# Attention in chunks of 64 tokens of two batches, in front of a gated MoE, on one core

## The chip, the core and the metric

The kernel runs on one core of a Trainium2 chip. The metric is the device time of one execution in microseconds (us), from runs on the chip; the profile is one execution more, recorded by the hardware profiler. The engines are TensorE (PE, and PEld for its weight loads), VectorE (DVE), ScalarE (ACT), GpSimd (POOL) and SyncE (SP, which issues the DMAs).

## The reference

Per batch and head a 48x48 state decays and grows with each token, and is read by the query. The result of all heads is a row of 384 numbers per token, which goes through two matrix products with a gate between.

```python
B, H, S, D = 4, 8, 768, 48
for t in range(S):
    state = alpha[:, :, t, :, None] * state + np.einsum('bhd,bhe->bhde', k[:, :, t], v[:, :, t])
    y[:, :, t] = np.einsum('bhd,bhde->bhe', q[:, :, t], state)
x = y.transpose(0, 2, 1, 3).reshape(B * S, H * D)      # 3072 x 384
h = x @ w_in                                           # 384 x 2048
g = h * tanh(softplus(h))
out = g @ w_out                                        # 2048 x 384
```

All is float32; the MoE weights arrive as 64-bit words and are taken apart on the chip.

## The kernel before

**Work.** The 3072 tokens are 24 chunks of 128 tokens of one batch, ordered by position and then batch, so chunk n continues the state of chunk n - 4. A MoE unit is one block f of 128 of the 2048 hidden columns for 2 or 4 chunks: nine matmuls up (`up`, L820, a float32 product as three passes over high and low parts), seven element-wise steps on ScalarE and VectorE (L829 to L855), and three matmuls down per chunk (`down`, L883), summed in a PSUM bank of the chunk. `SEGMENTS` fixes the order of the 106 units: 20 units of 2 chunks for chunks 0 to 7 and blocks 0 to 4, then units of 4 chunks. Units 20 to 24 are chunks 4 to 7 with blocks 5 to 9, units 25 to 35 chunks 0 to 3 with blocks 5 to 15, 36 to 41 chunks 4 to 7 with blocks 10 to 15, and from 42 on chunks 8 to 23. `weight` (L409) takes each of the 16 weight blocks apart, for w_in and w_out, on VectorE (L430, L435, L440, L459) and ScalarE (L445); for the first three blocks TensorE helps (L469, L470).

**A chunk of attention** (`attention`, L514). Four pairs of heads lie in 112 partitions: one head in rows 0 to 47, the other in rows 64 to 111. VectorE makes decay products by two scans (`scan_rest` L561, `scan_front` L578), scales the keys in two parts (`mult_k` L573) and the queries (`mult_q` L588), and decays the state (`decay` L593). TensorE makes the scores (`scores` L608): of the 128x128 causal square of each head only three 64x64 blocks, by 16 products of 48 rows in quarters of the array, half of them 128 and half 64 columns wide. VectorE copies the causal part to `probs` (`mask` L618), twice a chunk, 384 columns each. TensorE turns the keys by four transposes (`turn` L756), ScalarE copies them (L760). `product` is the y block: the past (state times queries, L633, 8 products of 48 rows and 128 columns in quarters), the late half's diagonal (L633, 8 products of 128 rows and 64 columns), the change of the state (L660, 8 products of 128 rows and 48 columns) and the early half's diagonal (L633, 8 products of 64 rows and 64 columns). Each float32 product is two instructions. A memset on GpSimd (L647) stands between the past and the early diagonal. The first chunk of a batch has no past, the last no turn and no change of state.

**After the y block.** ScalarE writes the high part of x (`upper` L687), VectorE the low part (`lower` L692); for chunks below `X_PE` = 8, TensorE subtracts (`off` L699) and ScalarE copies (`left` L707) instead. Six small DMAs a chunk move rows of x (`move` L713). VectorE adds the change to the state (`gather` L794), or ScalarE copies it in the first chunks (L792). A finished chunk's result goes from PSUM through ScalarE (`result` L917) into one store (L923). At the end a sum over all checks decides whether a general path must run (L996, L997).

**The order of the work** is written by a planner, `Plan.order` (L176): every task has an engine, a cost, a key and needs. An engine takes, of the tasks it may look at (`WINDOW`), the one that can begin first, and among equals the one with the lowest key. The keys come from due times (`due`, counted in units) and the tables `SHIFT`, the costs from `COST`. PSUM has eight banks: two "att", two "h" for `up`, and o0 to o3; `EARLY_BANKS` lends h and o banks to some chunks. q, k and alpha have two buffers, `rest` one. Where TensorE would wait before a planned time of 130 us, the planner puts in dummy matmuls (`fill`, L933).

## Time and profile before

| | |
|---|---|
| time, median of 3 runs | 509.16 us (509.13 to 509.31) |
| profiled execution, span from first to last instruction | 507.4 us |
| TensorE clock granted | 0.997 of full |
| instructions | 11433 |
| moved by DMA | 56.68 MB, mean 112 GB/s |

The profiled execution has no time of its own beside its span; the runs are 1.8 us above it, which is what lies before the first and behind the last instruction. In the rows, an engine's busy time counts overlapping matmuls once, and a matmul's length runs from its start to the end of its pipeline, so neighbours overlap: what a stretch of matmuls costs is read from its start to the start of the next one. A row with `x16` merges 16 instructions.

### The profile page before, as it was taken

What the parts mean: (1) busy time and instruction counts of PE and PEld (TensorE: products, weight loads), DVE (VectorE), ACT (ScalarE), POOL (GpSimd) and SP (SyncE); (2) the same over time, 40 slices, a digit from 0 to 9 for tenths busy, and PEclk for the clock granted to TensorE, in tenths of its full rate; (3) what the DMA queues carried; (4) which work ended last, traced back from release to release, by engine and by line L of the source; (5) the groups of instructions that cost most, each with busy time, mean ns of one, the idle gap of its engine ahead of it and who ended that gap; (6) DMA issues with size and microseconds to landing.
All of it is one profiled execution on the core that took longest, in us unless ns stands there. A gap on an engine that the chain in (4) does not pass through costs nothing.

```text
span 507.4 us, 11433 instructions
## 1 busy us (share of the span) xinstructions
PE 499.2 (98%) x4453; PEld 439.0 (87%) x4453; DVE 377.6 (74%) x729; ACT 391.1 (77%) x908; POOL 4.7 (1%) x34
## 2 busy tenths in 40 slices
PE   7999999999999999999999999999999999999996
PEld 4678899988988888889988888988989988999996
DVE  8999999999998897878557477867467654454442
ACT  2567799979879899969966955858866866887774
POOL 2000000000000000000000000000000000000000
PEclk9999999999999999999999999999999999999998
DMA  8656542525316685763220150220032000100001
GB/s 324 239 200 199 166 151 80 175 92 175 125 63 211 218 271 192 242 235 122 83 69 33 63 167 8 85 84 5 30 122 83 4 10 8 64 0 1 1 1 66
DMA packets 20074, 56.68 MB, mean 112 GB/s; under 512 B 4016, under 2 KB 12464, under 8 KB 20016
## 3 DMA queue, kind: packets, MB, share of 16 engines
q1 hardware_dynamic: 20016, 55.91, 32.4%
q8 instruction: 36, 0.59, 0.5%
q14 instruction: 22, 0.18, 0.1%
HBM read 48.82 MB, written 4.72 MB: 106 GB/s over the span
## 4 chain that ended last, share of the span: by engine, by line
PE 94%; DVE 4%; issue 1%; POOL 1%; ACT 0%; POOLq 0%
PE bank L883 40%; PE bank L820 40%; PE bank L633 7%; PE bank L608 3%; PE bank L660 2%; PE bank L756 1%; DVE rest L561 1%; DVE qka L578 1%; DVE probs L618 1%; PE bank L933 1%; DVE w_lead L435 0%; DVE qka L588 0%; PE bank L699 0%; PE bank L469 0%; DVE w_lead L440 0%
## 5 line engine op out<-in xcount | busy, mean ns | idle before, releaser
L883 PE MATMUL bank<-wo,g 128*128 128x384 f32 x1152 | 218.1, 339 | 0.0
L820 PE MATMUL bank<-xs,wi 128*128 128x512 f32 (+1 forms) x954 | 212.5, 372 | 0.1
L883 PEld LDWEIGHTS bank<-wo,g 128*128 128x128 f32 x1152 | 199.1, 188 | 5.6 <-issue 0.3
L820 PEld LDWEIGHTS bank<-xs,wi 128*128 128x128 f32 x954 | 167.0, 188 | 28.9 <-PE bank L883 0.4
L839 DVE SCALAR_TENSOR_TENSOR y<-u,bank 128x512 f32<-128x512 f32 (+1 forms) x106 | 66.8, 632 | 47.0 <-ACT u L829 46.8
L855 DVE TENSOR_TENSOR g<-t,g 128x512 fp32r<-128x512 f32 (+1 forms) x106 | 66.4, 637 | 32.3 <-ACT g L852 31.9
L852 ACT ACTIVATE g<-t 128x512 fp32r<-128x512 f32 (+1 forms) x106 | 60.8, 586 | 29.8 <-PE bank L883 26.5
L848 DVE SCALAR_TENSOR_TENSOR t<-y,t 128x512 f32<-128x512 f32 (+1 forms) x106 | 67.0, 634 | 21.4 <-ACT t L845 21.1
L829 ACT ACTIVATE u<-bank 128x512 f32<-128x512 f32 (+1 forms) x106 | 58.3, 550 | 30.2 <-PE bank L820 29.4
L842 ACT ACTIVATE t<-t,tenth 128x512 f32<-128x512 f32 (+1 forms) x106 | 71.6, 677 | 1.5
L835 ACT ACTIVATE t<-u 128x512 f32<-128x512 f32 (+1 forms) x106 | 62.0, 587 | 10.4 <-DVE g L855 9.6
L845 ACT ACTIVATE t<-t 128x512 f32<-128x512 f32 (+1 forms) x106 | 61.7, 584 | 0.7
L561 DVE TENSOR_TENSOR_SCAN rest<-qka,behind 112x516 f32<-112x516 f32 x24 | 29.5, 1228 | 1.9 <-DMA qka<-in_qka_dram 1.8
L618 DVE COPY_PREDICATED probs<-causal,bank 128x384 f32<-128x384 uint32 x48 | 25.9, 584 | 5.5 <-PE bank L608 5.5
L578 DVE TENSOR_TENSOR_SCAN qka<-qka,ahead 112x516 f32<-112x516 f32 x24 | 29.4, 1225 | 0.0
L687 ACT ACTIVATE xs<-bank 112x256 fp32r<-112x256 f32 x48 | 16.2, 378 | 15.6 <-PE bank L633 10.7
L633 PE MATMUL bank<-probs,v 128*64 128x64 f32 (+3 forms) x768 | 26.9, 227 | 0.2
L633 PEld LDWEIGHTS bank<-probs,v 128*64 128x64 f32 (+3 forms) x768 | 20.6, 128 | 6.3 <-issue 3.1
L608 PE MATMUL bank<-qka 48*64 48x128 f32 (+1 forms) x768 | 21.2, 248 | 0.2 <-DVE qka L588 0.2
L608 PEld LDWEIGHTS bank<-qka 48*64 48x64 f32 x768 | 18.2, 133 | 3.7 <-issue 1.9
L829 ACT ACTIVATION_READ_ACCUMULATOR u<-bank 128x1 f32 x106 | 20.6, 194 | 0.0
L573 DVE TENSOR_TENSOR qka<-qka,rest 112x256 f32<-112x256 f32 x48 | 19.2, 404 | 0.0
(79 smaller groups left out, 323.9 us busy)
## 6 DMA issues: line engine op xcount, KB each, us to landing
qka<-in_qka_dram SPq DMA_DIRECT2D x22, 770.5 KB, 4.8
ws<-in_wp_dram SPq DMA_DIRECT2D x16, 768.0 KB, 4.4
wc<-in_wp_dram SPq DMA_DIRECT2D x16, 768.0 KB, 4.7
v<-in_vp_dram SPq DMA_DIRECT2D x24, 192.0 KB, 4.5
out_dram<-osb SPq DMA_DIRECT2D x16, 192.0 KB, 1.9
xs<-xs SPq DMA_DIRECT2D x144, 16.0 KB, 2.1
out_dram<-part SPq DMA_DIRECT2D x8, 192.0 KB, 2.0
qka<-in_qka_dram SPq DMA_DIRECT2D x2, 258.5 KB, 3.5
```

What stands on the lines that cost most here:

```text
L608: nc.tensor.matmul(p[a][to, i, blocks], K()[r : r + D, j, to], q.rearrange("p (x t) -> p x t", t=HALF), start=True, stop=True,)
L633: return nc.tensor.matmul(p[m][64 * side : 64 * side + wide, j % 2, t], l(wide), r, start=j % 2 == 0 and lead, stop=stop, skip_group_check ...
L820: nc.tensor.matmul(p[:, :N], wi[:, z, s, fs], x[:, s, :, a], start=m == 0, stop=m == len(passes) - 1,)
L829: nc.scalar.activation(wide(u), wide(h), AF.Exp, scale=-1.0, accum_out=uchk[:, at : at + 1])
L835: nc.scalar.activation(wide(t), wide(u), AF.Square, bias=1.0, scale=2.0)
L839: nc.vector.scalar_tensor_tensor(wide(y), wide(u), 0.5, wide(h), ALU.add, ALU.mult)
L842: nc.scalar.activation(wide(t), wide(t), AF.Ln, bias=tenth, scale=0.1)
L845: nc.scalar.activation(wide(t), wide(t), AF.Exp, scale=-1.0)
L848: nc.vector.scalar_tensor_tensor(wide(t), wide(y), 0.4, wide(t), ALU.mult, ALU.mult)
L852: nc.scalar.activation(g.tile[:, 0, :N], wide(t), AF.Copy)
L855: late[mybir.EngineType.DVE] = nc.vector.tensor_tensor(g.tile[:, 1, :N], wide(t), g.tile[:, 0, :N].bitcast(F32), ALU.subtract)
L883: made = nc.tensor.matmul(o.tile[:, :DM], g.tile[:, a, j * C : (j + 1) * C], wo[:, z, f], start=begins and m == 0, stop=end and m == 2,)
```

## The change

A chunk is now 64 tokens of each of two batches; there are still 24 chunks of 128 rows, but two chains of 12 in place of four of 6, so chunk n continues chunk n - 2. The two batches' states lie side by side (384 columns in place of 192).

- Scores: two diagonal 64x64 blocks per pair and head, 16 products of 48 rows and 64 columns. Half of the past (`past(1)`, 8 products of 48 rows and 64 columns) is put in front of them, so scores now need the decayed state.
- y block: 16 diagonal products of 64 rows and 64 columns, the other half of the past (`past(0)`, 8 products), and 16 products of 64 rows and 48 columns for the change of the state. All are quarters of the array. The GpSimd memset is gone; the first diagonal product depends on the two masks.
- Banks: three a chunk instead of five. The two y banks hold scores, past, products and the change of the state; chunks 0 to 3 keep scores apart.
- VectorE: masks of 256 columns, keys in one instruction, decay of 384 columns, the state's change added in two pieces of 192. `X_PE` is 4.
- Each finished chunk is stored by two DMAs of 64 rows.
- The tables `EARLY_BANKS`, `SHIFT` and `COST` have new values, and `WINDOW` is 10**6.

Cut to its core; the functions' removed lines stand in the listing above.

```diff
...
-NCH = S // C
-QKA = (3 * C + 1) * NPAIR + 1
+NX = B // 2
+NBLK = S // HALF
+NSEG = 2 * NPAIR
+SEG = HALF + 1
+QKA = 2 * NPAIR * C + NSEG * SEG + 1
...
-    0: "o3 h att att o1".split(),
-    1: "att o0 o2 att att".split(),
+    0: "att o3 att h att".split(),
+    1: "o2 att h h att".split(),
...
-X_PE = 8
+X_PE = 4
...
-WINDOW = 150
+WINDOW = 10**6
...
+    "load v": (0.47, 0.82), "load w": (0.45, 2.51), "move": (0.6, 0.15), "store": (0.94, 0.75),
...
+    "state": (0.275, 0.4), "state0": (0.28, 0.35), "decay": (0.475, 0.6), "mask": (0.36, 0.5),
+    "scores0": (0.7, 0.8), "scores": (0.95, 1.05), "y0": (1.2, 1.3), "y": (1.45, 1.55),
+    "y last": (1.0, 1.1), "turn": (0.35, 0.58),
...
-    chunks = [(b, c) for c in range(NCH) for b in range(B)]
+    chunks = [(p, c) for c in range(NBLK) for p in range(NX)]
...
-    for b in range(B):
-        t = const.tile([R, NPAIR * D + P // 2 - D], F32, name=f"state{b}")
+    for b in range(NX):
+        t = const.tile([R, NSEG * D + P // 2 - D], F32, name=f"state{b}")
...
-        banks = EARLY_BANKS.get(n, ["att"] * 5)
-        bufs = [bank(z) for z in banks[:4]]
-        sc_buf, y_buf = bufs[:2], bufs[2:]
-        Q = lambda: by_pair(q_buf.tile[:R, : NPAIR * C])
-        K = lambda: by_pair(q_buf.tile[:R, NPAIR * C : 2 * NPAIR * C])
+        banks = EARLY_BANKS.get(n, ["att"] * 3)
+        y_buf = [bank(z) for z in banks[1:3]]
+        sc_buf = [bank(z) for z in banks[3:5]] or y_buf[::-1]
+        Q = lambda: by_half(q_buf.tile[:R, : NPAIR * C])
+        K = lambda: by_half(q_buf.tile[:R, NPAIR * C : 2 * NPAIR * C])
...
-        def mult_k(m):
-            def part():
-                k = K()[:, 2 * m : 2 * m + 2].rearrange("p j (x s) -> p j x s", x=2)
-                past = by_pair(rest.tile[:, 1:])[:, 2 * m : 2 * m + 2, 1:]
-                past = past.rearrange("p j (x s) -> p j x s", x=2)
-                nc.vector.tensor_tensor(k, k, past[:, :, :: -1 if m else 1], ALU.mult)
-            return part
+        def mult_k():
+            k = by_seg(q_buf.tile[:R, NPAIR * C : 2 * NPAIR * C])
+            nc.vector.tensor_tensor(k, k, by_seg(rest.tile[:, 1:])[:, :, 1:], ALU.mult)
 
...
+        of_state = st[:, : NSEG * D].rearrange("p (n e) -> p n e", n=NSEG)
+        by_head = st[:, : NSEG * D].rearrange("p (j x e) -> p j x e", j=NPAIR, x=2)
 
         def decay():
             nc.vector.tensor_tensor(
-                by_head, by_head, total().broadcast_to([R, NPAIR, D]), ALU.mult
-            )
+                of_state, of_state, total().broadcast_to([R, NSEG, D]), ALU.mult
+            )
+
+        SC = 2 * C
+        rows = lambda z: slice(HALF * z, HALF * z + D)
+        summed = lambda x: by_pair(within(y_buf[x])[:, :SC])
+        of_scores = lambda a: by_pair(within(sc_buf[a])[:, SC:])
+        change = lambda x: within(y_buf[x])[:, SC : SC + NPAIR * D].rearrange(
+            "p (j e) -> p j e", j=NPAIR
+        )
+
+        def head(j, a, x, start, weights, moving, stop=False):
+            side = 1 ^ a ^ (j // 2)
+            wide = D if side else HALF
+            return nc.tensor.matmul(
+                summed(x)[HALF * side : HALF * side + wide, j], weights(wide), moving,
+                start=start, stop=stop, skip_group_check=True,
+            )
+
+        def past(apart):
+            for i in range(2):
+                for j in (i, i + 2):
+                    for a in range(2):
+                        x, r = a ^ apart, rows(a)
+                        at = (2 * j + x) * D
+                        head(
+                            j, a, x, bool(apart) and i == 0, lambda w: st[r, at : at + w],
+                            Q()[r, j, x],
+                        )
 
         def scores():
...
+            if not first:
+                past(1)
+            leads = first or sc_buf[0] is not y_buf[1]
+            for j in range(NPAIR):
+                for x in range(2):
+                    for a in range(2):
                         nc.tensor.matmul(
...
+                            of_scores(a)[HALF * x : HALF * x + HALF, j], K()[rows(a), j, x],
+                            Q()[rows(a), j, x], start=leads and j == 0, stop=True,
+                            skip_group_check=True,
                         )
 
         slot = [(2 * n + a) % len(probs) for a in range(2)]
+        masked = [None, None]
 
         def mask(a):
             def part():
...
+                masked[a] = nc.vector.copy_predicated(probs[slot[a]], causal4, of_scores(a))
             return part
 
         def product():
...
+            leads = first and sc_buf[0] is not y_buf[1]
+            for i in range(2):
+                for a in range(2):
+                    for j in (i, i + 2):
+                        h = (2 * j + a) * D
+                        for x in range(2):
+                            part = slice(HALF * x, HALF * x + HALF)
+                            made = head(
+                                j, a, x, leads and i == 0 and a == 0,
+                                lambda w: V()[part, h : h + w], probs[slot[a]][part, j],
+                                stop=first and i == 1,
+                            )
+                            if i == j == a == x == 0:
+                                for z in masked:
+                                    tc.add_manual_dep(
+                                        made.ins, z.ins.name, SYNCED, reason="rows apart"
+                                    )
             if not first:
...
+                past(0)
+            if not last:
+                leads = sc_buf[0] is y_buf[1]
+                for j in range(NPAIR):
+                    for x in range(2):
+                        part = slice(HALF * x, HALF * x + HALF)
+                        for a, wide in ((0, HALF), (1, D)):
+                            h = (2 * j + a) * D
+                            nc.tensor.matmul(
+                                change(x)[HALF * a : HALF * a + wide, j],
+                                ks_buf.tile[part, j, HALF * a : HALF * a + wide],
+                                V()[part, h : h + D], start=leads and j == 0, stop=True,
+                                skip_group_check=True,
                             )
...
...
-        of = lambda m: by_slot(y_buf[m].tile)[:R]
-        to = lambda m, z: x[:R, 2 * m : 2 * m + 2, place, z]
+        of = lambda m: summed(m)[:R]
+        to = lambda m, z: x[:R, :, place, z, HALF * m : HALF * m + HALF]
...
-        t_k = [
-            add(
-                "DVE", *COST["half mult"], key + 0.03, mult_k(m), [t_rest, got_k], [q_buf, rest],
-                port=True,
-            )
-            for m in range(2)
-        ]
+        t_k = add("DVE", *COST["mult"], key + 0.03, mult_k, [t_rest, got_k], [q_buf, rest], port=True)
...
-        t_sc = add("PE", *COST["scores"], key + 0.2, scores, [*t_k, t_q], [q_buf, *sc_buf], small=(True, True))
+        t_sc = add(
+            "PE", *COST["scores0" if first else "scores"], key + 0.2, scores, [t_k, t_q, *t_decay],
+            [q_buf, *y_buf] + ([] if sc_buf[0] is y_buf[1] else sc_buf), small=(True, True),
+        )
...
-            [*t_mask, t_q, got_v, *t_decay] + ([] if last else [t_ks]),
-            [q_buf, v_buf, *y_buf] + ([] if last else [ks_buf]), small=(not first, True),
+            [*t_mask, t_q, got_v] + ([] if last else [t_ks]),
+            [q_buf, v_buf, *y_buf] + ([] if last else [ks_buf]), small=(True, True),
...
-        def gather():
-            u = y_buf[0].tile[:R, 2 * C : 2 * C + NPAIR * D].rearrange("p (j e) -> p j e", j=NPAIR)
-            if first:
-                nc.scalar.copy(by_head, u)
-            else:
-                nc.vector.tensor_tensor(by_head, u, by_head, ALU.add)
+        def gather(x):
+            def part():
+                u = change(x)[:R]
+                if first:
+                    nc.scalar.copy(by_head[:, :, x], u)
+                else:
+                    nc.vector.tensor_tensor(by_head[:, :, x], u, by_head[:, :, x], ALU.add)
+            return part
 
         done_state[b] = [
             add(
-                *(("ACT", *COST["state0"]) if first else ("DVE", *COST["state"])), key + 0.7,
-                gather, [t_y], [y_buf[0]],
-            )
+                *(("ACT", *COST["state0"]) if first else ("DVE", *COST["state"])),
+                key + 0.7 + 0.01 * x, gather(x), [t_y], [y_buf[x]],
+            )
+            for x in range(2)
         ]
-
 
...
-                nc.sync.dma_start(out[ds(b * S + c * C, C), :], osb.tile)
+                for x in range(2):
+                    nc.sync.dma_start(
+                        out[ds((2 * b + x) * S + c * HALF, HALF), :],
+                        osb.tile[HALF * x : HALF * x + HALF],
+                    )
...
+        a = inputs[name].reshape(NX, 2, NPAIR, 2, NBLK, HALF, D).transpose(3, 0, 4, 6, 2, 1, 5)
...
+    vp = inputs["v"].reshape(NX, 2, H, NBLK, HALF, D).transpose(0, 3, 1, 4, 2, 5)
+    vp = np.ascontiguousarray(vp).reshape(NX, NBLK, P, H * D)
...
```

## Rows read from the trace of the kernel before

**Rows 1.** The page, busy time and share of the span by engine.
```profile
PE 499.2 (98%) x4453; PEld 439.0 (87%) x4453; DVE 377.6 (74%) x729; ACT 391.1 (77%) x908; POOL 4.7 (1%) x34
```

**Rows 2.** The page, chain that ended last, shares by engine.
```profile
PE 94%; DVE 4%; issue 1%; POOL 1%; ACT 0%; POOLq 0%
```

**Rows 3.** Busy by stage: stage and length; PE, PEld, DVE, ACT, POOL; clock; DMA.
```profile
33.00:107.00 74.00, 73.85 (x828) 67.86 (x818) 72.28 (x170) 63.34 (x186) 0.35 (x4) 1.00 0.46 153
107.00:190.00 83.00, 83.00 (x744) 72.87 (x743) 77.13 (x152) 74.73 (x169) 0.49 (x4) 1.00 0.51 173
190.00:420.00 230.00, 229.84 (x2068) 204.12 (x2067) 158.27 (x280) 174.98 (x386) 1.06 (x12) 1.00 0.27 90
```

**Rows 4.** Timeline of PE: start, length, line, operation, count.
```profile
106.75 2.24 PE L820 MATMUL bank<-xs,wi 128*128 128x512 f32 x9
...
262.39 0.66 PE L633 MATMUL bank<-qka,state 48*48 48x128 f32 x16
262.98 0.68 PE L633 MATMUL bank<-probs,v 128*64 128x64 f32 x16
263.47 0.64 PE L660 MATMUL bank<-v,ks 128*48 128x48 f32 x16
264.04 0.46 PE L633 MATMUL bank<-probs,v 64*64 64x64 f32 x16
264.42 2.35 PE L883 MATMUL bank<-wo,g 128*128 128x384 f32 x12
```

**Rows 5.** Chain that ended last, in order of time, merged: start, length, what.
```profile
256.86 0.39 PE bank L756 x4
...
259.34 0.81 PE bank L608 x24
...
371.06 1.58 PE bank L633 x40
372.64 0.67 PE bank L608 x24
```

**Rows 6.** The same chain at an early chunk's two subtractions.
```profile
52.71 0.23 PE bank L699 x2
```

**Rows 7.** Groups of PE by shape: busy, mean ns, idle before.
```profile
L633 PE MATMUL bank<-probs,v 64*64 64x64 f32 x192 | 10.9, 230 | 0.0
```

**Rows 8.** Groups of DVE by shape: busy, mean ns, idle before.
```profile
L618 DVE COPY_PREDICATED probs<-causal,bank 128x384 f32<-128x384 uint32 x48 | 25.9, 584 | 5.5 <-PE bank L608 5.5
L573 DVE TENSOR_TENSOR qka<-qka,rest 112x256 f32<-112x256 f32 x48 | 19.2, 404 | 0.0
L588 DVE TENSOR_TENSOR qka<-qka 112x512 f32<-112x512 f32 x24 | 16.4, 683 | 0.0
L692 DVE TENSOR_TENSOR xs<-bank,xs 112x256 fp32r<-112x256 f32 x32 | 12.5, 417 | 5.1 <-ACT xs L687 5.1
L593 DVE TENSOR_TENSOR state<-state,rest 112x192 f32<-112x192 f32 x20 | 7.0, 350 | 0.0
L794 DVE TENSOR_TENSOR state<-bank,state 112x192 f32<-112x192 f32 x16 | 5.7, 356 | 5.3 <-PE bank L633 3.4 <-ACT xs L687 1.4 <-PE bank L699 0.6
```

**Rows 9.** Groups of PE by shape in the first 106.7 us.
```profile
L820 PE MATMUL bank<-xs,wi 128*128 128x256 f32 x180 | 24.6, 286 | 0.0
...
L820 PE MATMUL bank<-xs,wi 128*128 128x512 f32 x36 | 9.0, 393 | 0.0
```

**Rows 10.** Timeline of DVE: chunk 8's first scan, weight block 9's w_in part.
```profile
70.98 1.22 DVE L561 TENSOR_TENSOR_SCAN rest<-qka,behind 112x516 f32<-112x516 f32 x1
...
103.83 0.56 DVE L459 TENSOR_TENSOR wi<-w_lead,wi 128x384 fp32r<-128x384 f32 x1
```

**Rows 11.** The last stores: timeline, then line L923 (min/median/max ns of one issue).
```profile
501.67 1.89 SPq L923 DMA_DIRECT2D out_dram<-osb  x4
...
L923 SPq DMA_DIRECT2D out_dram<-osb x16: 332/333/714, 281.4 to 503.2; - x16
```

**Rows 12.** Groups of ACT by shape: busy, mean ns, idle before.
```profile
L829 ACT ACTIVATE u<-bank 128x512 f32<-128x512 f32 x86 | 50.7, 590 | 26.2 <-PE bank L820 25.4
```

194 lines of the change are left out of this document (59 added, 135 removed), and 39 rows, old and new, of the table SHIFT.

## The prediction

> **What bounds the kernel now.** I read the page's busy shares first [rows 1], then the chain of waits [rows 2], then the busy time by stage [rows 3]. TensorE is busy 98% of a span of 507.4 us, and the chain that ended last lies on TensorE for 94% and on VectorE for 4%. The stages tell where VectorE matters: between 33 and 107 us TensorE is busy 73.85 of 74 us, but VectorE also 72.28 of 74; between 107 and 190 VectorE has 77.13 of 83; from 190 to 420 it has 158.27 of 230, while TensorE is still full [rows 3]. So from about 107 us on, a microsecond less on TensorE is a microsecond less of time; before that, it is so only if VectorE can keep up.
>
> How a chunk of attention stands on TensorE is read from one chunk in the middle [rows 4] and from the merged chain [rows 5]. Scores take 0.81 us. The y block is four stretches: past (16 instructions, start 262.39), diagonal of the late half (262.98), state change (263.47), and the 64x64 diagonal (264.04), until the next MoE matmul starts at 264.42: 2.03 us. I fit these with one unit. Past and the 64x64 stretch have the same 16 instructions in four quarters, four rounds each, with 128 columns in one and 64 in the other: 0.59 against 0.38 us. The difference, 0.21 us over 4 rounds, is 0.053 us for a round of 64 columns, and 0.38 - 4 x 0.053 = 0.17 us is left as the price of one stretch of a shape. It gives 12 x 0.053 + 0.17 = 0.81 for the scores (4 rounds of 128 columns, 4 of 64), as measured, and 16 x 0.053 + 0.17 = 1.02 for the two 128-row stretches, against 264.04 - 262.98 = 1.06. Where 64x64 products were followed by scores, these took 0.67 [rows 5]: no 0.17 between 64-row and 48-row quarters.
>
> **The change on TensorE.** Everything becomes quarters, so scores and y are one stretch each. Middle chunk: scores now hold half of the past (8 products, 4 rounds) and 16 products of 64 columns (8 rounds): 12 x 0.053 + 0.17 = 0.81. The y block holds 16 diagonal products (8 rounds), the other half of the past (4) and 16 of the state change (8; 48 columns, taken at the full 0.053 since weights are up to 64 wide): 20 x 0.053 + 0.17 = 1.23. Together 2.04 against 0.81 + 2.03 = 2.84. First chunks: 8 and 16 rounds, 0.59 + 1.02; before, 0.81 and a y without past, 16 + 4 rounds and two stretches, 1.40. Last chunks: 0.81 + 12 rounds, 0.81; before 0.81 + 1.58 [rows 5].
> - Before: 24 x 0.81 + 4 x 1.40 + 16 x 2.03 + 4 x 1.58 = 63.8 us.
> - After (2 first, 20 middle, 2 last): 2 x 1.61 + 20 x 2.04 + 2 x 1.62 = 47.3 us: **-16.5**.
> - Two more chunks turn their keys (22, not 20) at 0.39 [rows 5]: +0.8.
> - X_PE 4 instead of 8: four chunks drop two subtractions each, 0.23 a chunk [rows 6]: -0.9.
>
> Sum -16.6, of which chunks 0 to 7 have 8 x 0.81 + 4 x 1.40 + 4 x 2.03 - (2 x 1.61 + 6 x 2.04) = 4.7 and the 0.9, so 5.6; chunks 8 to 23 have **11.0**. The number of returns from attention to MoE is the same, so they cancel.
>
> One rule speaks against this. The 32 score instructions in 0.81 us are 25 ns each, but the 64x64 stretch has a length of 0.46 with a mean instruction of 0.230 [rows 4, 7], so its 16 starts fit in 0.23 us, 15 ns apart; I take the rounds. The Trainium skill, "TensorE: Matmul & The Clock Gate", section "Wait — 56ns, not 53.3ns?", says that starts never come closer than about 25 ns however small the matmul; by that the middle chunk would have 128 instructions, 3.2 us. The trace's 15 ns contradict that for quarters.
>
> **The change on VectorE**, all prices from [rows 8]. For chunks 0 to 7:
> - keys: one 112x512 (0.683) for two 112x256 (2 x 0.404): 8 x -0.125 = -1.0.
> - masks of 256 columns for 384, twice a chunk. Not shown; bounds are 0.584 (no gain) and two thirds, 0.389. The 512- and 192-column rows differ by 0.333 over 320 columns, about 1.04 ns each, so 0.45: 16 x -0.135 = -2.2.
> - decay, 384 columns for 192, in six chunks instead of four. Bounds 0.350 and 0.683; by that slope 0.55: 6 x 0.55 - 4 x 0.35 = +1.9.
> - state change added in two pieces of 192, in six chunks instead of four: (12 - 4) x 0.356 = +2.8.
> - remainder of x for chunks 4 to 7, moved here from TensorE and ScalarE: 8 x 0.417 = +3.3.
>
> Together **+4.8 us** before the MoE units need it. Does it show? By 106.7 us, 20 half and 4 full units of MoE have begun: 180 and 36 up matmuls [rows 9]; the next, unit 24, begins at 106.75 [rows 4]. It needs the w_in part of weight block 9, which VectorE ends at 103.83 + 0.56 = 104.4 [rows 10]. TensorE alone would bring unit 24 to 106.75 - 5.6 = 101.1; VectorE alone to 104.4 + 4.8 = 109.2. But VectorE has already done chunk 8's preparation there (its scan runs at 70.98), whose result MoE needs only after 190: two scans, keys, q and decay, 2 x 1.22 + 2 x 0.40 + 0.68 + 0.35 = 4.3 us [rows 8, 10]. An order made anew can put that later: 109.2 - 4.3 = 104.9, so unit 24 comes **1.8 earlier**. I take this value, between 5.6 earlier and 2.5 later.
>
> After 107 us the added VectorE work (0.55 - 0.35 + 0.356 - 2 x 0.135 - 0.125 = 0.16 a middle chunk) goes into its idle time, 72 us between 190 and 420 [rows 3]. ScalarE loses eight evictions and gets nothing. POOL's memset between the two row halves goes; its wait covered nothing. Scores now also wait for decay; decay waits for the state of two chunks earlier, but the double-buffered q/k/alpha load already waits for that chunk's products, so it adds little. If that cover fails, score blocks and the mask queue behind them slip, and MoE units already prepared run in the gap.
>
> **The end.** Each result goes out in two stores: eight in place of four on SyncE after the last matmuls. Before, four take 1.89 us [rows 11], paced by ScalarE's results; one issue takes at least 0.332, and eight at some 0.4 end about 0.9 later: **+0.9** (0 to 1.5). The other 40 go into SyncE's idle time.
>
> **Sum.** Profile and runs differ by what lies around the span: 507.4 against a median of 509.16, so 1.8 us, unchanged. 509.2 - 11.0 - 1.8 + 0.9 = 497.3; I say **497.3**.
>
> **Rivals.**
> - VectorE keeps up everywhere, TensorE's whole saving shows: 509.2 - 16.6 + 0.9 = 493.5. For: the chunk 8 work done too early; against: 72.28 of 74 us. Chance 0.18.
> - VectorE sets the pace to unit 24 with nothing moved: 509.2 - 11.0 + 2.5 + 0.9 = 501.6. Chance 0.14.
> - Banks: y banks now hold scores, past and products until the state is gathered, so the table lends MoE's "h" banks oftener for longer; each loan can make one up wait for the two steps that free the other bank, the exponential (0.59 [rows 12]) and a VectorE step of 512 columns (0.68 [rows 8]). At some 10 loans, 12 us: about 509. Against: VectorE idles later [rows 3]. Chance 0.02.
> - The other side, the change not doing what it says: quarters don't overlap four wide, starts come 25 ns apart as the scores' mean has it [rows 4, 5]. Middle chunks cost 128 x 0.025 = 3.2, first ones 2.4, last ones 2.4: 2 x 2.4 + 20 x 3.2 + 2 x 2.4 = 73.6 against 63.8, so 509.2 + 9.8 + 0.8 - 0.9 + 0.9 = 519.8. It decides from 2.84 / 128 = 22 ns on. Against: 15 ns [rows 4, 7]. The page of the Trainium skill named above would have it so. Chance 0.04.
>
> The forecast itself keeps 0.62. Low end: 493.5 and up to 3 us from a new order in the first 33 us, 490.5. High end: 501.6 and dearer quarters; the diff's own cost table gives 0.93 + 2.13 - 0.95 - 1.45 = 0.66 a middle chunk where I have 0.80, 20 x 0.14 = 2.8: 504.4. A measurement of this kernel can tell about 0.2%, 1 us. Faster: all but the last two rivals and a little, 0.93; same 0.02; slower 0.05.
>
> **What would show it.** Right: scores stretch near 0.8 and y block near 1.2 us to the next MoE start, one stretch without the 0.17 gaps; VectorE nearly full to 105 us and unit 24 near 105; TensorE full after that; VectorE's total near 385 us. Wrong: starts in quarters over 20 ns apart, TensorE idle before up matmuls on "h" banks, idle time after 107 us, or unit 24 after 109 us.

## The result: 512.55 us, 0.6% slower, and the profile after

The changed kernel takes a median of **512.55 us** (511.8 to 513.16, four runs) against 509.24 for the kernel before: ratio 1.0062, interval 1.0048 to 1.0076. Forecast were 497.3 us, range 490.5 to 504.4, and 0.93 for faster. The profiled execution took 512.09 us, with a span of 510.4.

The page's busy shares and the chain that ended last, answering to [rows 1, 2]:

```profile
PE 493.4 (97%) x5251; PEld 433.8 (85%) x5251; DVE 382.7 (75%) x738; ACT 388.5 (76%) x902; POOL 2.4 (0%) x12
...
PE 82%; DMA 6%; DVE 5%; ACT 3%; issue 2%; SPq 1%; DVEq 0%
```

TensorE has 5.8 us less to do and the span is 3 us longer. Before, the chain lay on TensorE for 94% and touched no DMA; now 6% of it, some 31 us, are transfers.

The stages of [rows 3] (stage and length; PE, PEld, DVE, ACT, POOL; clock; DMA):

```profile
33.00:107.00 74.00, 73.36 (x989) 67.59 (x990) 73.07 (x176) 63.66 (x183) 0.00 (x0) 1.00 0.46 151
107.00:190.00 83.00, 81.18 (x879) 72.13 (x877) 77.74 (x152) 69.09 (x157) 0.00 (x0) 1.00 0.43 138
190.00:420.00 230.00, 226.61 (x2487) 200.84 (x2487) 161.94 (x286) 180.50 (x396) 0.00 (x0) 1.00 0.32 105
```

From 107 to 420 us TensorE now idles 5.2 us, where it idled 0.2. The clock is full in every stage; it plays no part.

Attention itself, in TensorE's timeline (start, length, line, count), answering to [rows 4]. L605 holds past, diagonal and head products, L628 the scores, L669 the state change, L879 the down products:

```profile
226.45 0.46 PE L605 MATMUL bank<-qka,state 48*48 48x64 f32 x16
226.71 0.66 PE L628 MATMUL bank<-qka 48*64 48x64 f32 x32
227.30 1.34 PE L879 MATMUL bank<-wo,g 128*128 128x384 f32 x6
...
238.49 0.69 PE L605 MATMUL bank<-probs,v 64*48 64x64 f32 x32
238.97 0.44 PE L605 MATMUL bank<-qka,state 48*48 48x64 f32 x16
239.20 0.67 PE L669 MATMUL bank<-v,ks 64*48 64x48 f32 x32
239.80 1.49 PE L879 MATMUL bank<-wo,g 128*128 128x384 f32 x7
```

Scores take 227.30 - 226.45 = 0.85 us (forecast 0.81), y 239.80 - 238.49 = 1.31 (1.23): 2.16 a middle chunk, 2.04 forecast, 2.84 before. 128 matmul instructions in 2.16 us start 17 ns apart on average, so quarters do overlap, and the rival of 25 ns is out.

So the saving is real. To see where it went I added up, over all matmuls of a trace, the time from its start to the next one's start, and gave it to its line; MoE and weight products at their undisturbed pace (up 0.229 us for 512 columns, down 0.174, dummy 0.164), what they took beyond it as "waits and switches". The third column is the kernel half_stores_half_check of below, in which the stalls are gone.

| us on TensorE, from its first matmul to the first one behind the last down | before | after | stalls taken away |
|---|---|---|---|
| attention (of it ahead of 33 us) | 63.3 (9.1) | 52.4 (6.4) | 50.6 (6.4) |
| dummies | 9.0 | 13.9 | 13.9 |
| turns of keys | 7.8 | 8.3 | 7.9 |
| subtractions of x | 2.6 | 1.9 | 1.9 |
| MoE and weight products | 404.4 | 404.4 | 404.4 |
| waits and switches of shape | 13.9 | 19.6 | 16.6 |
| sum | 501.0 | 500.5 | 495.5 |

Attention lost 10.8 us, 2.7 of them ahead of 33 us, where nothing is gained: the first up product starts at 32.92 us instead of 33.14, and dummies fill the place. Their group in the first 33 us, in the kernel before and after:

```profile
L933 PE MATMUL bank<-behind 112*128 112x384 bf16 x51 | 12.3, 376 | 2.6 <-DVE behind L349 2.6
```
```profile
L933 PE MATMUL bank<-behind 112*128 112x384 bf16 x79 | 16.8, 355 | 2.4 <-DVE behind L352 2.4
```

The last down ends at 502.00 us, before at 502.58 (first row; the second is the changed kernel's): of all that was saved 0.6 us is left there.

```profile
494.10 8.48 PE L883 MATMUL bank<-wo,g 128*128 128x384 f32 x48
```
```profile
493.49 8.51 PE L879 MATMUL bank<-wo,g 128*128 128x384 f32 x48
```

And then the end loses 3.6: 510.4 - 502.0 = 8.4 us from the last down to the span's end, before 507.4 - 502.58 = 4.8. SyncE's timeline there, answering to [rows 11]:

```profile
501.08 5.71 SPq L920 DMA_DIRECT2D out_dram<-osb  x8
```

Eight stores take SyncE 5.71 us from the first to the last, where four took 1.89. Seven of the eight issues take 0.47 to 0.60 us, the last 1.36; the four of before took 0.33 each and waited for ScalarE's results in between.

The other loss is between 165 and 215 us. SyncE's queue (L920 stores, L490 loads for the weight check, L533 and L542 a chunk's q/k/alpha and v, L709 moves of x), first in the kernel before, then after:

```profile
177.36 1.51 SPq L923 DMA_DIRECT2D out_dram<-part  x3
...
191.57 7.57 SPq L488 DMA_DIRECT2D wc<-in_wp_dram  x3
203.00 1.37 SPq L923 DMA_DIRECT2D out_dram<-part  x2
```
```profile
173.20 5.05 SPq L920 DMA_DIRECT2D out_dram<-part  x6
...
193.15 10.62 SPq L490 DMA_DIRECT2D wc<-in_wp_dram  x3
203.95 5.74 SPq L920 DMA_DIRECT2D out_dram<-part  x8
209.79 0.53 SPq L490 DMA_DIRECT2D wc<-in_wp_dram  x1
210.43 0.37 SPq L533 DMA_DIRECT2D qka<-in_qka_dram  x1
```

A row of the queue counts SyncE's waits between its issues too. The issues alone, as count and min/median/max ns, are these in the same stretch, before and then after:

```profile
L923 SPq DMA_DIRECT2D out_dram<-part x8: 343/392/525, 177.4 to 210.5; - x8
```
```profile
L920 SPq DMA_DIRECT2D out_dram<-part x16: 467/541/942, 173.2 to 209.2; - x16
```

Eight issues of 128 rows sum to 3.3 us, sixteen of 64 rows to 9.0: a store of half the rows holds SyncE longer, not shorter. The weight check loads wait for their buffer in the same queue, and the next chunk's q/k/alpha stands behind both.

A wait costs the queue more still. In both traces each of SyncE's DMAs (251 before, 275 after) signals on the semaphore of the DMA eight places ahead of it, and is not issued until that one has landed. So a queue with twice as many stores reaches less far ahead in the work. The q/k/alpha load at 187.16 us follows the landing, at 187.10, of the one issued at 178.98, eight places ahead, after 2.4 us without an issue. Between 165 and 220 us SyncE's waits of this kind are these (us in total, times, longest) and one of 0.2:

```profile
SPq L533 <- DMA qka<-in_qka_dram: 3.6, 2, 2.3
SPq L920 <- DMA wc<-in_wp_dram: 1.8, 2, 1.5
SPq L542 <- DMA v<-in_vp_dram: 1.2, 1, 1.2
SPq L709 <- DMA qka<-in_qka_dram: 1.0, 1, 1.0
```

Together they are 7.8 us; the kernel before has none there. (A check load's wait for the load whose buffer it takes, 4.5 us and before 4.0, is not counted.) What all that does is in the chain and then in TensorE's timeline (bracket: idle time before, and what ended it):

```profile
180.54 7.03 DMA v<-in_vp_dram
...
193.15 5.54 DMA wc<-in_wp_dram
...
203.45 5.76 DMA wc<-in_wp_dram
209.23 0.99 ACT wc L499 x2
```
```profile
211.09 0.57 PE L750 MATMUL bank<-ident,qka 112*128 112x112 f32 x4 [1.16 <-DVE xs L688]
```

A late check load holds ScalarE, which is in order, at its check (L499); what ScalarE should do behind it, x for the next MoE units (L683), comes late, and TensorE idles.

### The profile page after: what moved, and what is told of

The parts are those of the page before. It is cut to its first block, busy times and chain, and to the rows that moved or that the text cites. A ratio compares the mean times of both kernels' runs of the same rounds, so it can differ in the third digit from the quotient of the medians.

```text
span 510.4 us, 13018 instructions
## 1 busy us (share of the span) xinstructions
PE 493.4 (97%) x5251; PEld 433.8 (85%) x5251; DVE 382.7 (75%) x738; ACT 388.5 (76%) x902; POOL 2.4 (0%) x12
## 4 chain that ended last, share of the span: by engine, by line
PE 82%; DMA 6%; DVE 5%; ACT 3%; issue 2%; SPq 1%; DVEq 0%
PE bank L816 35%; PE bank L879 33%; PE bank L605 4%; PE bank L933 3%; DMA qka<-in_qka_dram 3%; DMA wc<-in_wp_dram 2%; PE bank L628 2%; PE bank L750 2%; PE bank L669 1%; DMA v<-in_vp_dram 1%; PE bank L471 1%; SPq L709 1%; DVE rest L559 1%; DVE y L835 1%; DVE qka L568 1%
## 5 line engine op out<-in xcount | busy, mean ns | idle before, releaser
L879 PE MATMUL bank<-wo,g 128*128 128x384 f32 x1152 | 219.4, 339 | 1.2 <-DVE g L851 0.8
L879 PEld LDWEIGHTS bank<-wo,g 128*128 128x128 f32 x1152 | 200.6, 188 | 7.8 <-DVE g L851 1.6
L559 DVE TENSOR_TENSOR_SCAN rest<-qka,behind 112x520 f32<-112x520 f32 x24 | 29.7, 1236 | 6.6 <-DMA qka<-in_qka_dram 6.6
L572 DVE TENSOR_TENSOR_SCAN qka<-qka,ahead 112x520 f32<-112x520 f32 x24 | 29.6, 1235 | 0.0
L683 ACT ACTIVATE xs<-bank 112x256 fp32r<-112x256 f32 x48 | 15.8, 378 | 13.9 <-PE bank L669 5.7
L605 PE MATMUL bank<-qka,state 48*48 48x64 f32 (+1 forms) x704 | 20.2, 222 | 0.6 <-DVE y L835 0.3
L605 PEld LDWEIGHTS bank<-qka,state 48*48 48x48 f32 (+1 forms) x704 | 15.4, 127 | 5.8 <-issue 4.2
L933 PE MATMUL bank<-behind 112*128 112x384 bf16 x85 | 18.0, 353 | 2.4 <-DVE behind L352 2.4
L639 DVE COPY_PREDICATED probs<-causal,bank 128x256 f32<-128x256 uint32 x48 | 18.9, 442 | 0.7 <-PE bank L628 0.5
L605 PEld LDWEIGHTS bank<-probs,v 64*48 64x48 f32 (+1 forms) x768 | 13.4, 127 | 6.4 <-issue 2.2
L688 DVE TENSOR_TENSOR xs<-bank,xs 112x256 fp32r<-112x256 f32 x40 | 15.2, 418 | 3.2 <-ACT xs L683 3.1
```

Source lines behind the costliest of these rows:

```text
L559: nc.vector.tensor_tensor_scan(t[:, :0:-1], alpha()[:, :0:-1], behind[:, ::-1], 0.0, ALU.mult, ALU.max)
L605: return nc.tensor.matmul(summed(x)[HALF * side : HALF * side + wide, j], weights(wide), moving, start=start, stop=stop, skip_group_check= ...
L879: made = nc.tensor.matmul(o.tile[:, :DM], g.tile[:, a, j * C : (j + 1) * C], wo[:, z, f], start=begins and m == 0, stop=end and m == 2,)
```

## The experiments

**Theory A**: the doubled stores in SyncE's queue turned the saving round. **Theory B**: the new order put the loads for the weight check where they stall the queue; the stores matter only at the end. Runs 8 to 12 look for a store without the fault, 13 and 14 price it in the change itself, 15 to 17 ask what is left when the order is made anew.

**1. one_store.** A chunk's result in one DMA.

```diff
-for x in range(2):
-    nc.sync.dma_start(out[ds((2*b+x)*S + c*HALF, HALF), :], osb.tile[HALF*x : HALF*x+HALF])
+to = out.rearrange("(z s) d -> z s d", s=S)[2*b : 2*b+2]
+nc.sync.dma_start(to[:, c*HALF : c*HALF+HALF], osb.tile)
```

> The changed kernel with one store for a finished chunk, 128 rows with the two batches' 64 rows as two pieces of one DMA; the order of all other work is the same. Theory A (the second store of each chunk clogs SyncE's queue): the eight last stores of the changed kernel hold SyncE from 501.08 to 506.79 us, the four of the kernel before ended at 503.56, so about 2.7 us come back at the end, and most of the slip of some 6 us between 165 and 215 us too, where loads of q/k/alpha and v stand behind stores: 503.5 to 506 us in all. Theory B (the new order puts weight-check loads, chunk loads and moves too close together, whatever the stores do): only the end comes back, 509 to 510.5 us.

555.19 us, ratio 1.0889 (1.0859 to 1.0919). Both theories missed. SyncE's timeline shows four such stores, and the DMA view from 212.7 to 221.4 us, in 40 slices, the busy share of the 16 engines in tenths and GB/s:

```profile
212.67 8.71 SPq L920 DMA_DIRECT2D out_dram<-part  x4
```
```profile
DMA  0994458969998322021111111111111111111411
GB/s 0 132 198 113 113 226 339 367 254 367 395 424 339 141 113 85 35 85 71 57 56 42 56 42 56 42 56 42 56 56 42 56 42 56 42 57 42 132 49 49
```

While only stores are under way, about a tenth of the engines' time is used, some 50 GB/s. The Trainium skill, "DMA: Bandwidth & Descriptors", section "Why a DMA increments its semaphore by 16 and not by 1", says that a DMA uses the largest number of engines, up to 16, that divides the slowest dimension of both its patterns; here one of them is 2, and 2 of 16 agrees with the row. A store in a poor shape is worse than two in a good one, and later versions put 64 outermost.

**2. half_check_loads** and **3. before_two_stores.** The first loads and checks only the w_in half of a weight block; the second is the kernel before with each store in two.

```diff
# half_check_loads
-t.rearrange("p m c w -> p (m c w)"),
-w[f].rearrange("p m c -> p (m c)").bitcast(I32),
+t.rearrange("p m c w -> p (m c w)")[:, : 2 * DM],
+w[f].rearrange("p m c -> p (m c)").bitcast(I32)[:, : 2 * DM],
...
# before_two_stores
-nc.sync.dma_start(out[ds(b*S + c*C, C), :], osb.tile)
+for x in range(2):
+    nc.sync.dma_start(out[ds(b*S + c*C + x*HALF, HALF), :], osb.tile[x*HALF : x*HALF+HALF])
```

> The changed kernel with the weight check loading and checking only the w_in half of each block (384 KB instead of 768 KB; the check of w_out is left out), two stores as they are. Theory A: the loads are not the cause, within 1.5 us of the changed kernel's 512.55. Theory B: the loads of 5.5 us that ScalarE and SyncE's queue wait for between 165 and 215 us are halved and the slip goes: 506.5 to 508.5 us.

> The kernel before with each store cut into two DMAs of 64 rows, nothing else. Theory A: the end grows by 2.7 us as in the changed kernel, and SyncE's queue is fuller in the middle, where this kernel had little slack between 190 and 210 us: 512 to 516 us. Theory B: only the end grows, 511.5 to 512.5 us.

half_check_loads: 507.31 us (0.9976, 0.995 to 1.0002), 5.2 less than the change. before_two_stores: 516.25 (1.0136, 1.0119 to 1.0153), 7.0 more than the kernel before. The same rows in each, last down products and last stores:

```profile
491.74 5.02 PE L879 MATMUL bank<-wo,g 128*128 128x384 f32 x28
...
495.84 6.13 SPq L920 DMA_DIRECT2D out_dram<-osb  x8
```
```profile
497.11 8.48 PE L883 MATMUL bank<-wo,g 128*128 128x384 f32 x48
...
504.68 5.83 SPq L924 DMA_DIRECT2D out_dram<-osb  x8
```

With half the check loads the last down ends at 496.76, 5.2 earlier than in the change, and the end stays long. With doubled stores in the kernel before, the last down ends at 505.59, 3.0 later, and the end is 3.7 longer. Each theory holds a part.

**4. one_store_half_check**, **5. pair_stores**, **6. pair_stores_half_check**, **7. before_half_check.** one_store with half the check loads; the change with the results of two chunks of a pair of batches in one tile and 24 stores of 64 partitions with two rows each; that with half the check loads; the kernel before with half the check loads.

```diff
# pair_stores
-nc.sync.dma_start(out[ds((2*b+x)*S + c*HALF, HALF), :], osb.tile[HALF*x : HALF*x+HALF])
+to = out[ds((2*b+x)*S + c//2*C, C), :]
+nc.sync.dma_start(to.rearrange("(j s) d -> s j d", j=2), pairs[z][HALF*x : HALF*x+HALF])
```

> Both edits on the changed kernel: one store for a chunk, and half the weight-check loads (the check of w_out is left out). Theory A: as with one store alone, 503.5 to 506 us, the loads add less than 1 us. Theory B: 503.5 to 506 us as well, but 4 us or more below one store alone. If neither takes the slip away, it stays at 509 to 510.

> The changed kernel, whole computation, in its own order, but the results of two chunks of the same two batches stand in one tile and leave together: a store is 64 partitions with two rows of two consecutive chunks each (128 rows, 192 KB), so 24 stores instead of 48, each spread as finely as before. Theory A (the number of DMAs in SyncE's queue): the end comes back by 2 to 3 us and most of the slip between 165 and 215 us: 504 to 507 us. Theory B (weight-check loads): only the end, 509.5 to 510.5 us.

> The same with the weight check loading only half of each block (the check of w_out is left out). Both suspects gone. Theory A and B alike: the last matmul ends near 495 us as with half the check loads alone, and the end is as short as in the kernel before: 502.5 to 504.5 us. A value above 506 would say that something else holds the changed kernel.

> The kernel before with half the weight-check loads (the check of w_out is left out): what the loads cost where the queue holds 24 stores. Theory A: nearly nothing, 508 to 509.3 us, since they were in time there. Theory B: as much as in the changed kernel, some 5 us, 504 us.

one_store_half_check 549.0 us (1.0777). pair_stores 511.35 (1.0047, 1.0033 to 1.0061), with half the check loads 507.96 (0.997, 0.9942 to 0.9998). before_half_check 509.31 (1.0001, 0.9992 to 1.0011): in the kernel before the check loads cost nothing, so theory B names something that the change alone has. It isn't that more of them stand there: from 165 to 215 us the kernel before issues 9 check loads among 44 DMAs, the change 6 among 55. Halving the number of stores took only 1.2 us, less than either theory expected. The end stayed long, 508.2 - 499.85 = 8.3 us from the last down, though four stores are issued there instead of eight: they land 2.8 to 4.5 us after their issue, the last at 506.42 us, where half_stores' four (below) land after 2.1 to 2.2. Why these land late is not shown.

**8. interleaved_store** and **9. interleaved_moving.** One store whose outer dimension is 64 needs the result's rows in the order (token, batch). The first writes x interleaved; the second leaves x and lets the up product read it interleaved.

```diff
+to = out.rearrange("(z s) d -> s z d", s=S)
+nc.sync.dma_start(to[c*HALF : c*HALF+HALF, 2*b : 2*b+2], osb.tile)
...
# interleaved_store
-to = lambda m, z: x[:R, :, place, z, HALF*m : HALF*m+HALF]
+to = lambda m, z: x[:R, :, place, z, m:C:2]
...
# interleaved_moving
-p[:, :N], wi[:, z, s, fs], x[:, s, :, a], start=m == 0,
+p[:, :N], wi[:, z, s, fs], x[:, s, :, a].rearrange("p n (x s) -> p n s x", x=2), start=m == 0,
```

> The changed kernel with one thing altered: the columns of a chunk's activations are interleaved (token, batch) where they are moved into a slot, so that row 2s+x of the result is token s of batch x, and a chunk's result leaves in one DMA whose outer dimension is the 64 tokens (24 stores instead of 48; the earlier one-DMA version had an outer dimension of 2 and took 555 us). Order, banks, engine work and loads are those of the changed kernel. Theory A (the doubled stores in SyncE's queue, at the end and in the crowd of 165 to 215 us, are what turned the saving round): the end comes back to before's (6.3 us behind the last down instead of 9.9) and the slip between 170 and 215 us shrinks by half or more, 503 to 507 us. Theory B (the weight check loads placed into that crowd are the cause, the stores only cost at the end): 3.6 less at the end alone, 508.5 to 509.5. Theory C (the slowness of one_store was not its outer dimension but one DMA taking 128 rows from two places): over 520 us.

> The changed kernel with one thing altered: the up products read a chunk's 128 columns of the activations interleaved (token, batch) as their moving operand, so that every later row order is 2s+x, and a chunk's result leaves in one DMA whose outer dimension is the 64 tokens (24 stores instead of 48). The writes of the activations stay as they were (in interleaved_store they were strided, and ScalarE then waited 28.8 us for moves of the activations, which hid the answer). Order, banks, loads and all other work are those of the changed kernel. Theory A (the doubled stores in SyncE's queue, at the end and in the crowd of 165 to 215 us, turned the saving round): the end comes back to before's 6.3 us behind the last down instead of 9.9, and the slip between 170 and 215 us shrinks by half or more: 503 to 507 us. Theory B (the weight check loads put into that crowd are the cause, the stores only cost at the end): 508.5 to 509.5. Theory C (a strided moving operand is read slower): the up products of 512 columns take more than their 374 ns, and each ns more adds 1 us over the 954 of them: the time is above 515 and the page shows that mean.

interleaved_store: 534.58 us (1.0477, 1.0454 to 1.05), and no answer: its waits show a new one, which the change doesn't have, for moves of x.

```profile
ACT xs L683 <- DMA xs<-xs: 28.8, 10, 4.5
```

Why the strided writes wait for those moves was not followed up. interleaved_moving: **502.44 us** (0.9864, 0.9848 to 0.9881), 10.1 below the change. Its last four stores and one row of ups between downs, and the same rows of ups and downs in the change:

```profile
494.37 2.48 SPq L922 DMA_DIRECT2D out_dram<-osb  x4
...
430.12 2.10 PE L818 MATMUL bank<-xs,wi 128*128 128x512 f32 x9
432.06 2.27 PE L881 MATMUL bank<-wo,g 128*128 128x384 f32 x12
```
```profile
435.15 2.24 PE L816 MATMUL bank<-xs,wi 128*128 128x512 f32 x9
437.23 2.27 PE L879 MATMUL bank<-wo,g 128*128 128x384 f32 x12
439.34 4.28 PE L816 MATMUL bank<-xs,wi 128*128 128x512 f32 x18
```

Two things had changed. The stores are cheap again, the end 500.7 - 495.29 = 5.4 us. And nine ups take 432.06 - 430.12 = 1.94 us instead of 437.23 - 435.15 = 2.08: start to start 216 ns instead of 231; what is new in them is that two neighbouring columns are read 256 bytes apart.

**10. interleaved_two_stores**, **11. before_interleaved**, **12. interleaved_both** part these two and carry the second on: interleaved_moving with two stores of every second partition; the kernel before with only the interleaved read; interleaved_moving with the down products reading w_out interleaved too.

```diff
# interleaved_two_stores
+for x in range(2):
+    nc.sync.dma_start(out[ds((2*b+x)*S + c*HALF, HALF), :], osb.tile[x:P:2])
...
# interleaved_both
-o.tile[:, :DM], g.tile[:, a, j*C : (j+1)*C], wo[:, z, f],
+o.tile[:, :DM], g.tile[:, a, j*C : (j+1)*C], wo[:, z, f].rearrange("p (y x s) -> p y s x", y=3, x=2),
```

> interleaved_moving with its store split in two again: one DMA of 64 rows for each batch, from every second partition, so that SyncE issues 48 stores as in the changed kernel, while the up products still read their moving operand interleaved. This parts the two things that interleaved_moving altered at once. It took 502.44 us, 10.1 less than the changed kernel's 512.55, and its trace has an unlooked-for thing: matmuls of the up product in a row start 216 ns apart instead of 230 (954 of them: 13 us of TensorE). Theory A (the stores): the gain is the stores', the trace's last down falls back by 5 or more, the end by 3, and the time is 509 to 512. Theory P (the pace): the gain is the quicker up products; only the end is lost again (3 to 3.6): 505 to 506.5. Between them, 507 to 509, both count.

> The kernel before with the up products' moving operand read interleaved in the same way (a chunk's columns 0, 64, 1, 65, ...) and its one store of 128 rows written with the 64 pairs outermost; nothing of the change is in it. Theory P (the interleaved read is quicker whatever the attention does): the up products start 216 ns apart here too, 13 us of TensorE less, and since TensorE bounds this kernel from 33 us on, 5 to 10 us off 509.2 (what the stretches bound by VectorE and the loads don't take back): 499 to 504. Theory A (the pace is worth nothing because the order is fixed and other engines set it): 508 to 510. This is also the fair base for interleaved_moving.

> interleaved_moving with the down products' moving operand (w_out) read interleaved as well (columns 64 apart in turn), and the sums straightened where they are copied from the banks. The down products of 384 columns start 173 to 174 ns apart in every kernel so far, while the dummies, with as many columns but in bf16, start 163.7 apart. If what an interleaved read saves is a matter of the read of the moving operand as such, the down products come to 163 ns as well: 1152 x 10 = 11.5 us less of TensorE; of that what VectorE, ScalarE and the loads leave: 493 to 499. If it is special to the activations (VectorE and ScalarE write them while they are read): 173 stays, 502 to 503. If the banks' copies with a step of 2 words are slower, ScalarE's result copy shows it, at most 1 us at the end.

interleaved_two_stores 509.61 us (1.0006, 0.9988 to 1.0024), before_interleaved 505.7 (0.9929, 0.9916 to 0.9943), interleaved_both 503.44 (0.9873, 0.9852 to 0.9893). So of the 10.1 us, about 2.9 are the quicker ups and **7.2 the stores**, much as the 7.0 in the kernel before. The read is worth 3.5 us in the kernel before as well: against 505.7 the change with a whole store, 502.44, is a gain of 3.3. In interleaved_both the downs quicken too, twelve in 437.38 - 435.43 = 1.95 us instead of 2.11, yet the time does not fall; 15 and 16 test whether the order, made for slower products, spends it on waits.

```profile
435.43 2.11 PE L885 MATMUL bank<-wo,g 128*128 128x384 f32 x12
437.38 4.38 PE L822 MATMUL bank<-xs,wi 128*128 128x512 f32 x18
```

**13. half_stores** and **14. half_stores_half_check** price the stores in the change itself, by leaving out the second of two.

```diff
-for x in range(2):
+for x in range(1):
```

> The changed kernel with the second of a chunk's two stores left out: the rows of a chunk's second batch are computed and not written (24 stores of 64 rows instead of 48; output incomplete). Nothing else is altered, the up products' pace neither, so this prices the doubled stores in the changed kernel itself. Theory A (the second store costs what it cost in the kernel before, +7.0, and between the two interleaved kernels, +7.2): 505 to 506, of it 3 at the end and the rest out of the slip between 170 and 215 us. Theory B (only the end): 508.5 to 509.5. Theory C (what costs is not the second issue but rows leaving at 96 KB a time): 511.5 to 513, no gain.

> half_stores with the weight check's loads halved as in half_check_loads (its w_out half is neither loaded nor checked; output incomplete as in half_stores). If the two causes are separate, their gains add: 7 and 5.2 off 512.55, 500 to 501, and the attention's saving is all there but for what the dummies took ahead of 33 us. If they are one stall in which either alone suffices, the second gives little: 503.5 to 505. The forecast, 497.3, would need the dummies' share too.

half_stores 506.58 us (0.9943, 0.9922 to 0.9964), 6.0 below the change; its last four stores take 2.39 us and its last down ends at 500.63, so 3.1 come at the end and the rest from the stall. Both halves 505.12 (0.9921, 0.9899 to 0.9943): 7.4 together and not 5.2 + 6.0, so the stall is one. TensorE's last down then ends at 496.93, the same as with half the check loads alone (496.76). From the start of unit 24, ahead of every store, to the end of the last down the change takes 398.7 us, half_stores 395.3, half_check_loads 392.3 and both halves 392.5: shorter loads take the whole stall away, fewer stores a little over half of it. SyncE's waits for the DMA eight places ahead, between 165 and 220 us, go the same way: 7.8 us, 3.4, 0.5 and none.

**15. planned_anew**, **16. planned_anew_2** and **17. before_planned_anew**: interleaved_both with the kernel's cost table set to what the traces show and its shifts of chunks, units and weights made anew, twice; and the kernel before with the same reads and costs and shifts made anew in the same way.

```diff
-"store": (0.94, 0.75),
+"store": (0.55, 0.75),
...
-"down": (0.521, 0.79),
+"down": (0.491, 0.76),
...
-COST["up", _n] = (9 * (0.4333e-3 * _c + 0.009), 9 * (0.4333e-3 * _c + 0.009) + 0.205)
+COST["up", _n] = (9 * (0.4167e-3 * _c + 0.003), 9 * (0.4167e-3 * _c + 0.003) + 0.205)
```

> interleaved_both (one store of 128 rows a chunk, both MoE products reading their moving operand interleaved) with the costs in the kernel's table set to what the traces showed (up 0.216 us a matmul of 512 columns, down 0.163, a store 0.55 instead of 0.94 for two, VectorE's 512-column steps 0.03 longer, weight checks 1.0) and with the hand-written shifts of chunks, units and weights made anew for them, so that loads stand before the stores and checks that hold SyncE's queue. The computation is the reference's. Theory O (what interleaved_both lost, TensorE 20 us shorter than in the kernel before and only 5.7 us of time, is the order's: it was made for slower products and dearer stores): by the traces the least TensorE can do is 33 us to the first up product, 187 us of ups and 187 of downs at the new pace, 44 of attention, 8 of turns and subtractions, some 16 of switches between shapes, and 7 behind the last down, 482; with 2 in 100 lost to waits, 485 to 495. Theory E (VectorE and ScalarE bound it from here): 500 or more, with idle TensorE all along.

> As planned_anew, with another set of shifts made in the same way. It shows how much of the result hangs on one order: within 3 us of planned_anew if the costs are right, more if chance waits decide.

> The kernel before, its attention and its one store a chunk untouched, with both MoE products reading their moving operand interleaved and with costs and shifts made anew in the same way as planned_anew. Against planned_anew (491.76) and planned_anew_2 (491.55) it tells what the changed attention is worth when each kernel has a whole store, the same reads and an order of its own. Theory W (the change is worth what attention loses on TensorE behind the first 33 us, 54.1 to 44.2 us, less 1 for turns and up to 3 for switches): 5 to 10 us more, 496.5 to 502. Theory N (the change is worth nothing, its gain always goes into waits): 490.5 to 493.

planned_anew **491.76 us** (0.9663, 0.9638 to 0.9687), planned_anew_2 491.55 (0.9649, 0.9634 to 0.9664), before_planned_anew 494.17 (0.9706, 0.9687 to 0.9725). What interleaved_both had lost was the order's, so the fastest kernel of this study is the change with one whole store a chunk, interleaved reads and an order made for both. Of its 20.8 us below the changed kernel the change itself is not the cause: against a kernel before with the same reads and planning it is worth 2.4 to 2.6 us, about 0.5%: between the two expectations, more than nothing and less than the 5 to 10. The kernel before got only one new order (the two of the change are 0.2 apart) and keeps its own `WINDOW` and `EARLY_BANKS`, so how much of the 2.5 is the order's is not shown. The groups of dummies say where the rest stays, first 33 us and whole span, planned_anew and then before_planned_anew:

```profile
L939 PE MATMUL bank<-behind 112*128 112x384 bf16 x68 | 14.5, 355 | 2.4 <-DVE behind L349 2.4
...
L939 PE MATMUL bank<-behind 112*128 112x384 bf16 x125 | 26.0, 343 | 2.4 <-DVE behind L349 2.4
```
```profile
L940 PE MATMUL bank<-behind 112*128 112x384 bf16 x69 | 15.7, 368 | 2.6 <-DVE behind L346 2.6
...
L940 PE MATMUL bank<-behind 112*128 112x384 bf16 x78 | 17.8, 364 | 2.6 <-DVE behind L346 2.6
```

Behind 33 us planned_anew runs 125 - 68 = 57 dummies, the last at 116 us, before_planned_anew 9. The 48 more are 48 x 0.164 = 7.9 us of TensorE with nothing else to do, in the stretch in which VectorE is nearly full (72.6 of 74 us from 33 to 107 us, 80.4 of 83 behind it).

## Why the prediction was wrong

Between 497.3 and 512.55 lie 15.2 us. By the prediction's steps:

- **"The other 40 go into SyncE's idle time": wrong, 5.1 us.** SyncE is in order. Between 165 and 215 us it had no room: 16 stores' issues there took 9.0 us, eight took 3.3 before, loads that TensorE's work depends on stood behind them, and each DMA waited for the landing of the one eight places ahead, often a slow load. The price is the last down's 502.00 against 496.93 us with the stalls gone (6.3 from unit 24 on, since that execution came 1.2 later to unit 24). It isn't the stores' alone: the check loads, which cost the kernel before nothing, are needed for it, and without the second stores a little under half of it stays. I had named SyncE's queue only for the end and put its middle at nothing.
- **"+0.9" for the end: the mechanism right, the size off, +3.6.** I took 0.4 us a store from a smallest issue of 0.33, which was one of 128 rows; the eight of 64 rows start 0.51 to 0.70 us apart and the last takes 1.36, and half_stores shows four at 2.39.
- **"-16.5" for attention: -12.6** where no stall disturbs it. A middle chunk measured 2.16, not 2.04 (20 x 0.12 = 2.4); the rest is a kernel before that spent 63.3, not 63.8, and the first and last chunks. My 0.053 us a round came from two stretches of 16 instructions.
- **"Chunks 8 to 23 have 11.0": 5.5.** From 107 us on, with the stalls gone, attention falls by 8.0 us (41.8 to 33.8), the turns add 1.25, waits and switches 1.3. The returns to MoE that I let cancel may be among these; that was not parted.
- **Unit 24: earlier by 3.5, forecast 1.8, and worth nothing.** The count of ups begun by 103.27 us is again 180 and 36 [rows 9]; the next starts at 103.28. (With the stalls gone it starts at 104.48, 2.3 earlier.) But ups and downs done by 107 us are 55.1 us of TensorE in half_stores_half_check and 55.0 before: ups came ahead of downs, and the start of one unit does not show it. The 2.9 us that attention, turns and subtractions leave there from 33 us on go to weight products that now stand behind 33 us (1.8), to waits and switches at the half-size ups (1.2) and to dummies (0.3). That VectorE sets the pace there (73.07 of 74 us), as the second rival says, fits this and was not tested; that rival's price, unit 24 later by 2.5, did not come.

```profile
L816 PE MATMUL bank<-xs,wi 128*128 128x256 f32 x180 | 25.1, 286 | 0.4 <-DVE y L835 0.4
L816 PE MATMUL bank<-xs,wi 128*128 128x512 f32 x36 | 9.0, 393 | 0.0
```

The sum: 5.1 + 2.7 (the end) + 5.5 (11.0 less 5.5) + 1.8 = 15.1 of the 15.2.

Right were the overlap of the quarters and the VectorE prices. The masks take 0.442 (forecast 0.45) and the decay 0.548 (0.55):

```profile
L639 DVE COPY_PREDICATED probs<-causal,bank 128x256 f32<-128x256 uint32 x48 | 18.9, 442 | 0.7 <-PE bank L628 0.5
L590 DVE TENSOR_TENSOR state<-state,rest 112x384 f32<-112x384 f32 x22 | 12.0, 548 | 0.0
```

The rival of the banks did not show: up products waited 0.9 us in all on VectorE's y. The missing rival was a queue: I gave the slower side 0.05 and looked for its cause on the engines only.

## What to carry to other kernels

Count every DMA that a change adds at every place in its queue, not only at the end, and ask which load stands behind it; an in-order queue has idle time only where nothing behind is due, and where only so many DMAs may be under way, one slow load holds up all that follow. Time saved on the bounding engine where another sets the pace is worth nothing, and the start of one unit is not the work done by then. When a change makes work cheaper, the order has to be made for the new costs, those of the queues too, before its worth can be read.

## What the runs showed of the hardware that was not expected

- A matmul whose moving operand is fp32 in 512 neighbouring columns starts every 230 ns or so (224 to 241), and every 216 when neighbouring columns are read 256 bytes apart; for 384 columns 173 to 174 and 163. It holds in both kernels and for activations and weights. The Trainium skill, "TensorE: Matmul & The Clock Gate", section "Wait — 56ns, not 53.3ns?", gives N / 2.4 GHz + 2.5 ns, 215.7 for 512 columns; the interleaved read agrees with it, the plain one is 14 ns over. Why is not shown.
- The issue of a store of 64 rows holds SyncE 0.47 to 1.59 us (48 in the changed kernel), that of one of 128 rows 0.33 to 0.71 (24 in the kernel before).
- A DMA of 128 rows with an outer dimension of 2 leaves at some 50 GB/s (one_store).
- In both kernels SyncE issues no DMA before the one eight places ahead has landed; in the changed kernel it stood 7.8 us for this between 165 and 220 us. Whether the program or the chip sets the eight is not shown.
